# Windowed attention and an MLP mixer on one core: score groups issued one by one instead of in 18 fixed bursts, with new issue orders

## The chip, the cores and the metric

The kernel runs on one core of one Trainium2 chip. The core has a matrix engine (TensorE, in the profile PE, its weight loads PEld), a vector engine (VectorE, DVE), a scalar engine (ScalarE, ACT), a general engine (GpSimd, POOL) and a sequencer that issues transfers (SyncE, SP). The metric is device time in microseconds (us); lower is better. The time given for a kernel is the median of several runs.

## What is computed

Four batches, eight heads, 768 positions, head size 64. Attention keeps, for each query, the first 4 keys (the sinks) and the 128 keys up to its own position. Its result, with the heads side by side as 512 channels, goes through a mixer: a two-layer product over positions (width 256) with a skip connection, then one over channels (width 1536) with another.

```python
scores = scale * np.matmul(q, k.transpose(0, 1, 3, 2))
keep = (pos[None, :] < n_sink) | ((rel >= 0) & (rel < window))     # n_sink 4, window 128
a = softmax(np.where(keep, scores, -1e9))
x = np.matmul(a, v)                        # to [4, 768, 512]
h = np.maximum(x.T @ w_tok1, 0.0) @ w_tok2
u = x + h.T
out = u + np.maximum(u @ w_ch1, 0.0) @ w_ch2
```

## The kernel before

Queries, keys and values are cast to bf16. The 32 heads are worked off as 16 pairs p of two heads, four pairs to a batch. For a pair the scores are computed transposed (keys by queries) in three groups g of two key tiles each, as three diagonal stripes of the window. Each group fills a slot of two PSUM banks, of which there are two (`sc`); four more banks (`mx`) serve everything else. ACT takes the exponential, DVE or POOL masks it, and PE multiplies it with the values.

**Units.** All work of PE is cut into units, each a short run of matmuls whose results other engines then fetch. A unit is named by a letter and a number; the letters are streams:

- first phase (pairs 0 to 3, batch 0): `t` transposes q and k, `m` writes the mask into PSUM, `s` scores, `o` products with the values (and one product with the sinks, o0), `g` and `h` the token mixer of batch 0 (two mix_h units, three mix_u units, three transpositions in each).
- later (pairs 4 to 15): `a` scores and what goes with them, `v` products with the values (two units a pair, v0 and v1 for pair 4), `k` the token mixer of batches 1 to 3, `c` the first channel product (c0 to c23 for batch 0, 42 units for each other batch), `x` and `y` the second channel product.

The string `ORDERED` lists all units in the order in which PE gets them; `plan.run` walks through it. PE executes in that order and no other, so a unit whose operands are late holds up all units behind it.

**The planner.** All other operations (copies out of PSUM, exponentials, masks, transfers) are put into the program between the units by `class Plan`, when the kernel is built: it keeps a clock for each engine, adds fixed costs, and emits the operation that can begin first. The times in it only decide the order of instructions on DVE, ACT, POOL and SP and on which of them an operation goes; on the chip each instruction waits for its own operands. For a load it takes a landing time: the queue's own time plus `RECEIPT`, and it lets `LANES` loads be on their way before the next is issued. `choose` picks PSUM banks for a unit and keeps, in `held`, who reads them.

**Loads.** The string `LOADS` gives the order in which POOL issues the loads from pair 4 on: `q4`, `k4`, `v4` and so on of a pair, `t1` and `t2` the token weights `w_tok1` and `w_tok2`, `c0` to `c3` quarters of `w_ch1`, `d0` to `d3` quarters of `w_ch2`. One queue takes them in that order. For pairs 8 to 15 q and k are transposed by a DMA that SP issues (line 542) once the load has landed; for pairs 4 to 7 PE transposes them.

**Forms.** A score matmul of pairs 4 to 15 has 64 rows and 64 columns of weights ("quarters": four run side by side), a sink product 64 by 32 ("eighths"), the first phase's scores 64 by 128 ("halves"); all else is 128 by 128 ("full"). The planner charges `SWITCH` for a change of form.

**Bursts.** In the stream `a` of before, a0 and a1 are the transpositions of q and k of pair 4. The 36 score groups of the 12 later pairs are taken two by two, which gives a2 to a19: a burst holds the transposition of the next pair by quarters (pairs 5 to 7), two groups, and the sink product of two pairs or the transposition of a batch's u by quarters where one falls due, sorted by form. So a burst needs both `sc` slots. In program order:

```python
for n in range(0, len(groups), 2):
    pieces = [x for k in range(3) for g in groups[n:n + 2] for x in (g[k] if k != 1 else [g[k]])]
    pieces.sort(key=lambda x: x.form)
    units.append(burst(*pieces))
```

Nearly all matmuls go through one helper and have line 187; transpositions have lines 158, 162, 190 and 584. Other lines: 172 loads of q and k (pairs 8 on), 180 of v, 205 of weights; 680 the exponential; 691 and 699 masks; 196 copies by DVE or POOL; 194 copies by ACT; 1471 and 1509 sums of weights; 1216 sums of the hidden layer; 1262 sums into the output tile.

Of the kernel before, what the change touches and what calls it, by code (L numbers as in the profile page):

```python
# [17 lines left out]
def kernel(  # L18
# [43 lines left out]
    )  # L62
    LOADS = (
        "q4 v1 t1 k4 v2 t2 v3 k5 q5 k6 q6 c0 v4 c3 c2 v5 q7 v6 k7 q9 c1 k9 q8 d3 k8 d1 v7 v11 d0 k10 d2 v8 "
        "k11 v10 v9 q10 k13 q11 q13 k12 q12 q15 v12 q14 k14 k15 v14 v13 v15 "
# [25 lines left out]
    LATER = "cxyakv"  # L91
# [204 lines left out]
    LANES = 8  # L296
# [3 lines left out]
    RECEIPT = 1500.0  # L300
    BIAS = 400.0
# [6 lines left out]
    class Op:  # L308
        def __init__(self, cost, fn, deps=(), then=(), size=0.0, lag=None, loads=0, traffic=0.0):
# [6 lines left out]
            self.need = {}  # L316
            self.first = self.last = 0
# [7 lines left out]
    class Plan:  # L325
# [57 lines left out]
        def other(self):  # L383
            best = None
            queue = False
            for n, op in enumerate(self.pending):
# [10 lines left out]
                e = min(op.cost, key=lambda e: max(self.free[e], r) + op.cost[e] + BIAS * (e == "DVE"))  # L397
                t = max(self.free[e], r)
# [6 lines left out]
        def commit_pe(self, op, t):  # L405
            given.update(self.choose(op)[1])
            for tag, banks in op.need.items():
                for n, readers in zip(given[tag], banks):
                    for m in (2 * n, 2 * n + 1) if tag == "sc" else (n,):
                        self.held[m] = readers  # L410
# [14 lines left out]
        def run(self, units, early):  # L425
# [3 lines left out]
            while units or self.pending:  # L429
# [3 lines left out]
                if o is not None and (t is None or o[0] <= t):  # L433
# [3 lines left out]
                    op.done = self.free[o[2]] + op.lag  # L437
                    if op.traffic:
# [572 lines left out]
    def attention_and_tokens():  # L1011
# [9 lines left out]
        units += [turn(first, n) for n in range(2)]  # L1021
        for p in range(first, last + 1):
# [3 lines left out]
            with_first, with_second = [], []  # L1026
            if p + 1 < min(BY_DMA, last + 1):
                with_first.append(transposed(p + 1))
            groups.append((with_first, scores(p, 0), [], sink_rows(p)))
            if p % 2:  # L1030
                groups[-1][2].append(sinks.pop())
            groups.append(([], scores(p, 1), with_second, None))
            groups.append(([], scores(p, 2), [], None))
            if p % 2 == 0:
                sinks = [score_sinks(p + 1)]
            if hp == NHP - 1 and p < BY_DMA:
                groups[-1][2].append(turned_u(b, 0))
# [548 lines left out]
```

## Time and profile before

| what | value |
|---|---|
| median of 3 runs | 195.54 us (192.81 to 198.23) |
| the profiled execution | 194.1 us, of it the span of its instructions 192.1 us |
| PE matmul busy | 180.8 us, 94% of the span, 2270 instructions |
| DVE busy | 161.1 us (84%) |
| ACT busy | 109.1 us (57%) |
| POOL busy | 81.9 us (43%) |
| granted TensorE clock | 1.0 throughout |

Times in the profile count from the first instruction of the span. A row of the timeline gives the start, the time from the start of the first to the end of the last instruction of the group, the engine, line, operation, out<-in with the shape of the weights and of the moving operand, the count, and in brackets the engine's idle time before it with what released it. Matmuls are pipelined: a row is longer than the time for which it keeps the next one from starting, so start times are compared, not lengths.

### The profile page before, as it was taken

What the parts mean: (1) busy time and instruction counts of PE and PEld (TensorE: products, weight loads), DVE (VectorE), ACT (ScalarE), POOL (GpSimd) and SP (SyncE); (2) the same over time, 40 slices, a digit from 0 to 9 for tenths busy, and PEclk for the clock granted to TensorE, in tenths of its full rate; (3) what the DMA queues carried; (4) which work ended last, traced back from release to release, by engine and by line L of the source; (5) the groups of instructions that cost most, each with busy time, mean ns of one, the idle gap of its engine ahead of it and who ended that gap; (6) DMA issues with size and microseconds to landing.
All of it is one profiled execution on the core that took longest, in us unless ns stands there. A gap on an engine that the chain in (4) does not pass through costs nothing.

```text
span 192.1 us, 5590 instructions
## 1 busy us (share of the span) xinstructions
PE 180.8 (94%) x2270; PEld 132.9 (69%) x2273; DVE 161.1 (84%) x340; ACT 109.1 (57%) x205; POOL 81.9 (43%) x132
## 2 busy tenths in 40 slices
PE   6688979799999999999999999999999999999992
PEld 1345667467667778885776789876777887667881
DVE  4466667697999799999999999989999986699953
ACT  4698858998896551528955760767453111773000
POOL 7198856497865398994262493040000000000000
PEclk9999999999999999999999999999999999999999
DMA  5999999999999999999999996250211204400144
GB/s 177 252 309 193 187 197 194 178 179 173 152 167 151 122 116 144 167 143 281 158 147 125 151 116 136 109 218 3 58 29 27 55 3 164 164 3 0 55 138 139
DMA packets 82601, 26.32 MB, mean 137 GB/s; under 512 B 70032, under 2 KB 80272, under 8 KB 82576
## 3 DMA queue, kind: packets, MB, share of 16 engines
q0 software_dynamic: 56864, 11.80, 77.6%
q1 hardware_dynamic: 25136, 13.64, 36.3%
q10 hardware_dynamic: 576, 0.52, 0.8%
q8 instruction: 18, 0.29, 0.6%
q14 instruction: 7, 0.06, 0.1%
HBM read 26.75 MB, written 6.29 MB: 172 GB/s over the span
## 4 chain that ended last, share of the span: by engine, by line
PE 60%; DMA 30%; DVE 3%; POOL 2%; issue 2%; SPq 0%
PE ps L187 60%; DMA w_ch<-in_moe_w_ch_dram 19%; DMA q_f<-in_q_dram 7%; DMA w_tok<-in_moe_w_tok_dram 4%; DVE q_f L1471 1%; DVE v_sums L1216 1%; POOL k_bf L172 1%; DVE o_sb L1262 1%; POOL v_aug L180 1%; DVE pT L699 1%; POOL w_ch L205 1%; SPq L135 0%; POOL q_bf L196 0%; PE ps L584 0%
## 5 line engine op out<-in xcount | busy, mean ns | idle before, releaser
L680 ACT ACTIVATE pT<-ps 128x1024 bf16<-128x1024 f32 (+1 forms) x48 | 44.0, 956 | 13.7 <-PE ps L187 13.6
L194 ACT ACTIVATE parts<-ps 128x384 f32<-128x384 f32 x54 | 24.4, 493 | 26.7 <-PE ps L187 22.5
L187 PE MATMUL ps<-uT,w_ch 128*128 128x384 bf16 x168 | 34.0, 326 | 0.1
L187 PEld LDWEIGHTS <-v1T 128*128 128x128 bf16 x288 | 27.8, 98 | 5.9 <-DVE q_f L1471 0.5
L1150 DVE CUSTOM_DVE_ANT_0 v1T<-ps,parts 128x384 bf16<-128x384 f32 x54 | 28.6, 552 | 3.4 <-PE ps L187 2.5
L187 PEld LDWEIGHTS <-w_ch 128*128 128x128 bf16 x204 | 19.3, 98 | 11.0 <-issue 0.6
L200 ACT ACTIVATE v1T<-ps 128x384 bf16<-128x384 f32 x39 | 18.9, 495 | 8.6 <-PE ps L187 8.0
L187 PEld LDWEIGHTS <-v_sums 128*128 128x128 bf16 x216 | 20.8, 98 | 3.0 <-issue 0.6
L187 PE MATMUL ps<-uT_sums,k_f 128*128 128x384 bf16 x108 | 22.6, 326 | 0.0
L187 PEld LDWEIGHTS <-w_tok 128*128 128x128 bf16 x192 | 18.4, 98 | 4.4 <-issue 0.5
L691 POOL TENSOR_SCALAR_AFFINE_SELECT pT<-pT 128x256 bf16<-128x256 bf16 (+1 forms) x28 | 15.0, 569 | 13.4 <-issue 9.3
L180 POOL DMA_DIRECT2D v_aug<-in_v_dram x16 | 17.0, 1063 | 7.0 <-PE ps L187 3.6
L187 PE MATMUL ps<-q_f,v1T 128*128 128x256 bf16 x144 | 19.2, 273 | 0.3 <-DVE q_f L1471 0.2
L187 PEld LDWEIGHTS <-k_f 128*128 128x128 bf16 x144 | 13.7, 98 | 7.7
L187 PE MATMUL ps<-w_ch,v1T 128*128 128x256 bf16 x144 | 19.0, 273 | 0.0
L187 PE MATMUL ps<-v_aug,pT 128*128 128x65 bf16 x352 | 18.0, 194 | 1.0 <-DMA v_aug<-in_v_dram 1.0
L1262 DVE TENSOR_TENSOR o_sb<-ps,u_sb 128x512 f32<-128x512 f32 (+1 forms) x32 | 17.1, 548 | 1.9 <-PE ps L187 1.9
L187 PEld LDWEIGHTS <-pT 128*128 128x128 bf16 x352 | 16.1, 98 | 3.2 <-DMA v_aug<-in_v_dram 1.3
L187 PE MATMUL ps<-q_f,v_sums 128*128 128x256 bf16 x144 | 18.2, 273 | 0.2 <-DVE o_sb L1262 0.2
L769 DVE TENSOR_TENSOR x_sb<-ps,recip 128x384 bf16<-128x384 f32 x32 | 17.3, 552 | 0.6
L1262 DVE TENSOR_TENSOR o_sb<-ps,o_sb 128x256 f32<-128x256 f32 (+1 forms) x24 | 12.9, 551 | 3.4 <-PE ps L187 3.2
L172 POOL DMA_DIRECT2D k_bf<-in_k_dram x16 | 13.4, 840 | 5.0 <-DMA q_bf<-in_q_dram 2.7
(88 smaller groups left out, 293.3 us busy)
## 6 DMA issues: line engine op xcount, KB each, us to landing
v_aug<-in_v_dram POOLq DMA_DIRECT2D x16, 192.0 KB, 11.0
w_ch<-in_moe_w_ch_dram POOLq DMA_DIRECT2D x8, 384.0 KB, 10.0
out_dram<-o_sb SPq DMA_DIRECT2D x6, 512.0 KB, 2.8
out_dram<-o_sb SPq DMA_DIRECT2D x10, 256.0 KB, 2.8
q_f<-in_q_dram SPq DMA_DIRECT2D x4, 384.0 KB, 6.5
k_f<-in_k_dram SPq DMA_DIRECT2D x4, 384.0 KB, 6.8
q_bf<-in_q_dram POOLq DMA_DIRECT2D x16, 96.0 KB, 8.3
k_bf<-in_k_dram POOLq DMA_DIRECT2D x16, 96.0 KB, 10.7
```

The source lines that it names most:

```text
L172: in_order(nc.gpsimd.dma_start(out=out[:, h], in_=rows[:, h]))
L180: in_order(nc.gpsimd.dma_start(out=v_aug.rearrange("p i t d -> p (i t) d")[:, :, 0:D], in_=v[b].rearrange("h s d -> (h s) d")[2 * hp * S:2 ...
L187: issue(nc.tensor.matmul(*args, skip_group_check=True, **kwargs))
L194: in_order(nc.scalar.activation(out, in_, AF.Copy))
L200: in_order(nc.scalar.activation(out, in_, AF.Relu))
L205: return in_order(nc.gpsimd.dma_start(out=out, in_=in_))
L680: in_order(nc.scalar.activation(part(tiles["pT", p][:, :, ds(2 * g, 2)]), of_keys(tiles["ps_s", p, g])[:, :, 0:width(g)], AF.Exp, scale=scale,
L691: in_order(nc.gpsimd.affine_select(out=pt, in_=pt, compare_op=ALU.is_ge, fill=0.0, base=-n, pattern=[[0, nk], [1 - 2 * n, P]], channel_mul ...
L699: in_order(nc.vector.tensor_tensor(out=pt, in0=pt, in1=m, op=ALU.min))
L769: in_order(nc.vector.tensor_tensor(out=x_sb[b][:, ts(half, QH), ts(hp, 2 * D)].rearrange("p t (i d) -> p t i d", i=2), in0=tiles["ps_o", p ...
L1150: in_order(nc.vector._custom_dve(TENSOR_ADD_SAT, out=v1_of(i, half), in0=ps, in1=kept[:, n], s0=HUGE, s1=0.0,))
L1262: in_order(nc.vector.tensor_tensor(out=sb(*out), in0=tiles["ps_out", b, t0, key[0]], in1=in1(), op=ALU.add,))
```

## The change

Each score group becomes a unit of the stream `a` (now a0 to a35, three to a pair). The transpositions by quarters get a stream `w` of their own: w0 and w1 for q and k of pair 4, w2, w3 and w4 for pairs 5 to 7, w5 and w6 for u of batch 1 (first and second half of its channels). The six sink products of two pairs become the stream `n`. The matmuls stay the same. `ORDERED` and `LOADS` are new strings.

In the planner `LANES` goes from 8 to 7, `RECEIPT` from 1500 to 2100 ns, and readers of one PSUM bank get a common record `reads`: an operation on another engine than the bank's last reader is taken to begin no earlier than 60 ns after that one's end.

```diff
@@ -46,23 +46,24 @@
 
 
     ORDERED = (
-        "t0-1 m0-1 s0-1 t2 m2 s2 t3 m3 s3 o0 m4 s4 t4 m5 o1 s5 t5 o2 m6 s6 t6 m7 s7 t7 o3 m8 s8 o4 a0 s9-10 m9 "
-        "g0-1 m10 a1 s11-12 o5-6 g2 o7-8 g3 a2 h0-1 g4-6 h2-3 a3 h4-6 g7 h7 c15 c0 c5 c10 a4 v0-1 c9 c6 c22 "
-        "v2-3 a5 c8 k0 c16 c7 c11 c3 c23 k1-2 a6 k3 c13 c1-2 c14 c18-19 a7 v4 c12 c20 v5 c17 v6 c21 v7 a8 x0 c4 "
-        "x1 k4 y0 a9 y2 x6-7 y3-4 x2 k5-6 x10 y5 x3 k7 v8 y6 x4-5 a10 x11 x8 c31 c24 x9 x12-13 v9-10 c27 c33 "
-        "c26 y1 c32 c29 v11 c34-35 a11 c28 c45 c36-37 c30 c47 c25 a12 c46 k8 c49 c48 a13 v12 c50 v13 c51 c41 "
-        "c38 k9 c39 c43 c40 c59 k10 v14-15 c52 c61 c42 c62 c54 c53 c63-64 c44 k11 c55-56 c65 c60 k12 c58 a14 "
-        "c57 x14 k13 x15 x18 a15 x19-21 a16 x22 y7 x24 k14 x25 v16 k15 x23 y8 x26-27 y9 v17 a17 v18 y10-11 v19 "
-        "a18 y12 x16-17 c73 a19 v20 y13 k16 c67 c66 c69 c75 v21 c76 c68 c77 c83 c71 c80 c78-79 c70 c82 c74 k17 "
-        "c81 c72 c85 k18 c94 c87 c84 c88 v22-23 c89 c86 k19 c96-97 c95 c90-91 k20 c101 c99 c92 c98 k21 c103-104 "
-        "c93 x28 c105 c100 c106 k22 c102 k23 y15 c107 x29 x32 y14 c115 x30-31 x34 x33 y17 x35 y16 c108 x36-39 "
-        "y19 c118 c117 y18 x40-41 y20 c119 c109 c111 c120 c110 c116 c113 c122 c132 c112 c129 c124 c130 c121 "
-        "c131 c114 c134 c125 c123 c126 c133 c136 c143 c127-128 c137 c145 c138 c135 c144 c139 c146 c140 c147 "
-        "x42-43 c141-142 c149 x44 x48 c148 x46 y21 x45 x47 x49 y24 y22 x50 x52-53 x51 y23 y26 x54-55 y27 y25"
+        "t0-1 m0-1 s0-1 t2 m2 t3 s2 m3 o0 s3 m4 s4 t4 o1 m5 s5 t5 o2 m6 t6 s6 m7 s7 t7 o3-4 m8 s8-10 w0 m9 g0 "
+        "m10 w1 s11-12 o5-6 g1 a0 o7 w2 a1-2 o8 g2-4 h0 g5 h1 a3 g6-7 h2-3 n0 h4-6 a4 v0-1 h7 c0 c5 c8 w3 a5 c3 "
+        "c7 c2 c18 a6 w4 a7 v2 c17 v3 c16 c20 c23 n1 c13 c21 a8-9 c15 k0 c22 c1 a10-11 c19 c12 c10 k1 c14 k2 "
+        "c11 c6 v4 k3 v5 x0-1 c4 v6 c9 v7 x2 a12-13 y0 k4 x3 x6 y3 y2 x7 a14 n2 a15 y5 y4 a16 k5 x10 v8 w5 a17 "
+        "x4-5 x11 v9 y6 y1 k6 x12 k7 v10-11 a18 w6 x13 c24 x8 c31 a19-20 k8 c26 x9 c34 c33 c32 c27 c36 c35 c25 "
+        "n3 a21 c28 k9 c29 c37 c39 c38 v12 a22 v13 k10 c30 c45 c40 c46 a23 c41 v14 c47 c59 c42 c48 c43 c49 v15 "
+        "c50 k11 c61 c44 c52 c51 c60 c62-63 c54 c53 c64 c55 k12 c57 c56 x14 k13-15 c65 c58 a24 x15-16 n4 a25-26 "
+        "y7 x17 x20 y8 x21 y10 y9 a27-28 x18-19 v16-17 y11-12 x24 v18 x25 y13 a29-30 x22 x26 c66 a31-32 x27 c73 "
+        "x23 c68 c67 v19 c74 c70 c75 c69 n5 a33 c77 c76 c71 k16 v20 c78 c80 a34 v21 c79 c72 k17 c87 c82 c88 c81 "
+        "k18 a35 c90 v22 c83-84 c89 c94 c92 v23 c85 c96 c91 c86 c101 k19-20 c102-103 c97 c93 c98 c104-105 x30 "
+        "c100 c106 c99 c95 x28 k21 c107 k22 y15 k23 x29 y14 c108 x32 x34 x31 x33 c115 x35 y17 y16 x36 x38-39 "
+        "y18-19 x37 x40 c118 x41 c110 c117 y20 c109 c120 c111 c122 c112 c116 c119 c113 c125 c124 c114 c123 c121 "
+        "c129 c127 c136 c132 c130 c126 c131 c137 c134 c143 c128 c133 c139 c138 c144-146 c135 c141 c140 c147 x42 "
+        "c148 x43-44 c142 c149 x46 x48 y21 x45 y22 x47 x49 y23-24 x50 x52-53 y25-26 x54-55 y27 x51"
     )
     LOADS = (
-        "q4 v1 t1 k4 v2 t2 v3 k5 q5 k6 q6 c0 v4 c3 c2 v5 q7 v6 k7 q9 c1 k9 q8 d3 k8 d1 v7 v11 d0 k10 d2 v8 "
-        "k11 v10 v9 q10 k13 q11 q13 k12 q12 q15 v12 q14 k14 k15 v14 v13 v15 "
+        "q4 v1 t1 v2 k4 v3 k5 q5 t2 c0 k6 v4 k7 c2 v5 q6 c1 q7 c3 d3 d2 d0 d1 q8 k8 v6 v7 k9 q9 v8 v9 k10 q10 "
+        "v10 k11 q11 k12 v11 k13 q12 q13 v12 k14 q14 k15 v13 q15 v14 v15 "
     )
     ORDER = (1, 2, 7, 6, 4, 5, 3)
     NQ = 6
@@ -88,7 +89,7 @@
 
     psum = ctx.enter_context(tc.tile_pool(name="psum", bufs=1, space=bass.MemoryType.PSUM))
     NSC, NMX = 2, 4
-    LATER = "cxyakv"
+    LATER = "cxyakvwn"
 
     given = {}
 
@@ -293,11 +294,11 @@
     PE_OUT = 200.0
     SWITCH = 95.0
     FIRST = 1800.0
-    LANES = 8
+    LANES = 7
     TURN, STORE = 1300.0, 700.0
     CROWDED = 1.7
     BLOCK = 1.4
-    RECEIPT = 1500.0
+    RECEIPT = 2100.0
     BIAS = 400.0
     FETCH, FETCH_ALONE = 7200.0, 4600.0
 
@@ -314,6 +315,7 @@
             self.urgent = 0
             self.loads, self.traffic = loads, traffic
             self.need = {}
+            self.reads = []
             self.first = self.last = 0
             self.after = None
 
@@ -394,8 +396,11 @@
                     r = max(r, self.landings[len(self.landings) + op.loads - LANES - 1])
                 if r is None:
                     continue
-                e = min(op.cost, key=lambda e: max(self.free[e], r) + op.cost[e] + BIAS * (e == "DVE"))
-                t = max(self.free[e], r)
+                at = {
+                    e: max([self.free[e], r] + [x[1] for x in op.reads if x[0] != e]) for e in op.cost
+                }
+                e = min(op.cost, key=lambda e: at[e] + op.cost[e] + BIAS * (e == "DVE"))
+                t = at[e]
                 if best is None or t < best[0] - 1e-6 or (
                     t < best[0] + 1e-6 and e == best[2] and op.urgent > self.pending[best[1]].urgent
                 ):
@@ -406,6 +411,9 @@
             given.update(self.choose(op)[1])
             for tag, banks in op.need.items():
                 for n, readers in zip(given[tag], banks):
+                    last = [None, 0.0]
+                    for r in readers:
+                        r.reads.append(last)
                     for m in (2 * n, 2 * n + 1) if tag == "sc" else (n,):
                         self.held[m] = readers
             first = count[0]
@@ -435,6 +443,8 @@
                     op.fn(o[2])
                     self.free[o[2]] = o[0] + op.cost[o[2]]
                     op.done = self.free[o[2]] + op.lag
+                    for x in op.reads:
+                        x[:] = [o[2], self.free[o[2]] + 60.0]
                     if op.traffic:
                         behind = max(0.0, self.queue - self.free["SP"])
                         crowded = behind > 1000.0
@@ -1018,23 +1028,23 @@
             tokens.extend(mix_u(b, g, st, 2) for st in range(0, NT, 2))
 
         prepare(first)
-        units += [turn(first, n) for n in range(2)]
+        turned = [turn(first, n) for n in range(2)]
         for p in range(first, last + 1):
             b, hp = pairs[p]
             if p < last:
                 prepare(p + 1)
-            with_first, with_second = [], []
+            with_second = []
             if p + 1 < min(BY_DMA, last + 1):
-                with_first.append(transposed(p + 1))
-            groups.append((with_first, scores(p, 0), [], sink_rows(p)))
+                turned.append(burst(transposed(p + 1)))
+            groups.append((scores(p, 0), [], sink_rows(p)))
             if p % 2:
-                groups[-1][2].append(sinks.pop())
-            groups.append(([], scores(p, 1), with_second, None))
-            groups.append(([], scores(p, 2), [], None))
+                groups[-1][1].append(sinks.pop())
+            groups.append((scores(p, 1), with_second, None))
+            groups.append((scores(p, 2), [], None))
             if p % 2 == 0:
                 sinks = [score_sinks(p + 1)]
             if hp == NHP - 1 and p < BY_DMA:
-                groups[-1][2].append(turned_u(b, 0))
+                groups[-1][1].append(turned_u(b, 0))
             out += [pv(p, half) for half in range(2)]
             if hp == 1 and p > NHP + 1:
                 tokens_of(b - 1, 1)
@@ -1043,12 +1053,14 @@
             if hp == 2:
                 tokens_of(b, 0)
         tokens_of(pairs[last][0], 1)
-        for n in range(0, len(groups), 2):
-            pieces = [x for k in range(3) for g in groups[n:n + 2] for x in (g[k] if k != 1 else [g[k]])]
-            pieces.sort(key=lambda x: x.form)
-            units.append(burst(*pieces))
-            units[-1].then.extend(g[3] for g in groups[n:n + 2] if g[3] is not None)
-        return units, tokens, out
+        sunk = []
+        for scored, others, rows in groups:
+            units.append(burst(scored))
+            if rows is not None:
+                units[-1].then.append(rows)
+            for x in others:
+                (turned if x.form == QUARTERS else sunk).append(burst(x))
+        return units, tokens, out, turned, sunk
 
     def mix_channels(b):
         units = []
@@ -1526,7 +1538,7 @@
     plan.pending.append(done["masks"])
 
     streams = dict(zip("smtohg", first_attention()))
-    streams.update(zip("akv", attention_and_tokens()))
+    streams.update(zip("akvwn", attention_and_tokens()))
     for b in range(B):
         for name, mixed in zip("cxy", mix_channels(b)):
             streams.setdefault(name, []).extend(mixed)
```

## The prediction

> **What bounds the kernel now.** I read the page's busy shares and slices first, then the chain that ended last, then the timeline of PE around every place where its starts are not evenly spaced.
>
> ```profile
> PE 180.8 (94%) x2270; PEld 132.9 (69%) x2273; DVE 161.1 (84%) x340; ACT 109.1 (57%) x205; POOL 81.9 (43%) x132
> PE   6688979799999999999999999999999999999992
> DMA  5999999999999999999999996250211204400144
> ```
> ```profile
> 50.01 16.86 DMA w_ch<-in_moe_w_ch_dram
> ...
> 73.10 5.32 PE ps L187 x65
> ...
> 78.85 109.67 PE ps L187 x1097
> ...
> 188.55 0.43 DVE o_sb L1262
> ```
>
> PE is busy in every slice and, from 73.1 us to 188.5, it is the chain by itself: more than 1,100 matmuls with nothing between them. There a unit can be put earlier or later without any gain, as long as PE never waits. Before that the chain is transfers (the last quarter of `w_ch2` lands at 66.9), and the PE slices fall below 9. So only two things can move the time: waits of PE before 73 us, and matmul time itself. The latter has a fixed part and a part that the order sets, the changes of form.
>
> The waits are found by comparing starts with the pace at which matmuls follow each other.
>
> ```profile
> 24.70 0.38 PE L187 MATMUL ps<-h1T,w_tok 128*128 128x256 bf16 x2
> 26.08 0.36 PE L187 MATMUL ps<-v_aug,pT 128*128 128x65 bf16 x6 [1.00 <-DMA v_aug<-in_v_dram]
> ...
> 27.75 0.38 PE L162 MATMUL ps<-ident,q_bf 64*64 64x64 bf16 x24
> ...
> 28.14 0.53 PE L187 MATMUL ps<-qT,kT 64*64 64x256 bf16 x16
> ```
> ```profile
> 32.27 0.56 PE L162 MATMUL ps<-ident,q_bf 64*64 64x64 bf16 x24
> ...
> 34.01 0.61 PE L187 MATMUL ps<-h1T,w_tok 128*128 128x256 bf16 x4
> 35.46 0.40 PE L190 MATMUL ps<-ident,u_sb 128*128 128x128 bf16 x4 [0.84 <-ACT qT L194]
> 36.18 0.83 PE L190 MATMUL ps<-ident,u_sb 128*128 128x128 bf16 x12 [0.32 <-DVE u_sb L919]
> 37.08 2.76 PE L187 MATMUL ps<-uT,w_ch 128*128 128x384 bf16 x16
> ```
> ```profile
> 50.67 0.49 PE L187 MATMUL ps<-h1T,w_tok 128*128 128x256 bf16 x3
> 51.10 0.52 PE L187 MATMUL ps<-qT,kT 64*64 64x192 bf16 x16
> 51.54 0.40 PE L187 MATMUL ps<-qT,kTs 64*32 64x512 bf16 x4
> 51.87 0.61 PE L187 MATMUL ps<-h1T,w_tok 128*128 128x256 bf16 x4
> ```
> ```profile
> 66.17 0.62 PE L187 MATMUL ps<-qT,kT 64*64 64x192 bf16 x16
> ...
> 67.51 0.83 PE L187 MATMUL ps<-q_f,v1T 128*128 128x256 bf16 x6 [0.22 <-DVE q_f L1471]
> 68.18 2.13 PE L187 MATMUL ps<-q_f,v_sums 128*128 128x256 bf16 x18
> 70.43 0.81 PE L187 MATMUL ps<-q_f,v1T 128*128 128x256 bf16 x6
> 71.25 0.81 PE L187 MATMUL ps<-w_ch,v1T 128*128 128x256 bf16 x6
> 71.90 1.04 PE L187 MATMUL ps<-h1T,w_tok 128*128 128x256 bf16 x8
> 73.10 0.27 PE L187 MATMUL ps<-q_f,v_sums 128*128 128x256 bf16 x1 [0.16 <-DVE o_sb L1262]
> ```
>
> Pace: six matmuls of 256 columns take 71.90 - 71.25 = 0.65, so 0.108 each; one of 128 columns is taken as half of that, 0.054. Now the waits, each a distance of starts less the work in it:
>
> - 24.70: 2 x 0.108 = 0.22, next start 1.38 later: **1.16**, for the values of pair 3.
> - 32.27 to 34.01 is 1.74. The 48 transpositions take 28.14 - 27.75 = 0.39, scores and sinks 51.87 - 51.10 = 0.77: **0.58**, within one burst that needs both score slots.
> - 34.01 to 35.46, four matmuls: **1.02**; to 36.18, four short ones: **0.50**; to 37.08, twelve: **0.25**. The transpositions of the token mixer wait, first until ACT has copied the transposed q of this burst out of a bank, then for the mixer's own results.
> - 66.17 to 67.51 against the same 0.77: **0.57**; 67.51 to 71.25, 30 matmuls (3.24): **0.50**; 71.90 to 73.10, eight (0.87): **0.33**. These are the first users of the last `w_ch2` pieces and of their sums.
>
> Together 4.9 us. That is the most that a better order could win from these places.
>
> **The change part by part.**
>
> *More changes of form.* Going by the strings, with the bursts taken apart into their forms, the old order changes form 68 times on PE, the new one 83 times (29 stretches of small matmuls become 37; n0 and n1 stand alone, n2 lies between two groups). The price is in the rows above: three full matmuls from 50.67 fill 0.32, the quarters start at 51.10, so going in costs 0.11. The last form starts at 51.54, its four sink products of 512 columns run side by side in 2 x 0.108, and the full matmul starts at 51.87: coming out costs 0.11. So 15 x 0.11 = **+1.65 us**, and this falls on PE where nothing hides it. Above it could be at most what a matmul shows beyond its columns: 0.40 long against 0.22 streamed, 0.18, so 15 x 0.18 = 2.7.
>
> The Trainium skill (TensorEngine Tiling (Array Packing), Tiling Modes) says that changing the tiling mode, not merely the tile, drains the engine, which speaks against the change; the rows agree with a cost but show 0.11 us. By the latency formula of TensorE: Matmul & The Clock Gate, Single matmul latency (398 cycles besides the columns, at 2.4 GHz), a full drain would be 0.166 us as an estimate, and the sum 0.8 us later.
>
> *Where the waits go.* In the new string o7 (values of pair 3) comes after a0 and g1, and v3 is loaded ahead of t2 instead of behind it, 2.0 us earlier by the rate below: the 1.16 goes. No transposition of q and k stands among h2 to h7 any more (w3 comes after c8), n0 lies between h3 and h4, and a4, v0 and v1 (1.2 us) ahead of h7: the 1.02, 0.50 and 0.25 go. A group no longer asks for two score slots at once: the 0.58 goes. The four `d` loads come as 20th to 23rd instead of within 24th to 31st; the last of them lands some 2.4 ahead of k8 (53.6 below), at 51, and x0, its first user, starts 4.2 ahead of a12 (62.2 below), at 58: the 0.57, 0.50 and 0.33 go. **-4.9 us.** I take all of it; the lower bound of this gain is nothing, if what comes next in order is late instead.
>
> *What is late next, early.* Loads are in one queue.
>
> ```profile
> 24.00:32.00 8.00, 7.00 (x150) 5.92 (x147) 5.24 (x15) 5.22 (x11) 4.45 (x6) 1.00 1.51 194
> 48.00:56.00 8.00, 8.00 (x70) 4.99 (x68) 7.61 (x15) 6.91 (x14) 6.99 (x11) 1.00 1.89 159
> ```
> ```profile
> v_aug<-in_v_dram POOLq DMA_DIRECT2D x16, 192.0 KB, 11.0
> w_ch<-in_moe_w_ch_dram POOLq DMA_DIRECT2D x8, 384.0 KB, 10.0
> ...
> w_tok<-in_moe_w_tok_dram POOLq DMA_DIRECT2D x2, 384.0 KB, 7.6
> ```
>
> The last column of the first two rows is GB/s. At 194 a load of 384 KB takes 2.0 us, one of 192 KB 1.0. Before, q5 landed by 27.75 at the latest (its transposition starts then), with t2 ahead of it. In the new order t2 comes behind q5: so q5 by 25.7 and t2 by 27.7. When are they wanted? g2, which needs t2, starts at 24.3 before (the two matmuls at 24.70 are its last). In front of it now stand in addition o7 and o8 (0.9), a0, a1 and a2 (together about 0.5), w2 (0.4) and, net of a merged stretch, one entry and exit (0.2): 26.3. So PE can wait up to 1.4 there, most of it already at w2; nothing, if t2 lands as much earlier as its queue had slack. All units are behind that wait. I take **+1.0 us**, nearer to the upper end, since sizes and rate are rows.
>
> *What is late next, at pair 8.* q8 comes 24th instead of 23rd, and k8 stays 25th, but of the first 25 loads three small ones (v6, q9, k9: 576 KB) are replaced by three large (d0, d1, d2: 1152 KB).
>
> ```profile
> 49.90 1.80 SPq L542 DMA_TRANSPOSE kT<-k_bf  x1
> ```
> ```profile
> 59.87 0.43 POOL L196 COPY kTs<-kT 64x4 bf16<-64x4 bf16 x2 [1.48 <-DMA kT<-k_bf]
> ...
> 65.42 0.82 POOL L172 DMA_DIRECT2D q_bf<-in_q_dram x1 [2.92 <-DMA k_bf<-in_k_dram]
> ```
> ```profile
> DMA to landing us min/median/max: 6.0/8.8/10.4
> ```
>
> Before, k8 was there at 49.9, when SP issued its transposition, and that landed 10 us later. 576 KB more at 159 GB/s are 3.7 us, so k8 at 53.6, and transposed between 59.6 and 64.0 (the last row is of the tile kT). Its first reader is a12.
>
> ```profile
> 61.66 0.54 PE L187 MATMUL ps<-qT,kT 64*64 64x256 bf16 x16
> ```
>
> Pair 8's scores began at 61.66 before. Without the waits ahead of them (3.5), with x0 to x2 (2.0), one more c unit of four 384-column matmuls (0.65), and seven more changes of form net of one transposition of u that comes later (0.4), they stand at 61.2, with the early wait at 62.2. So PE waits 0 to 1.8 there; I take **+0.5**. What is queued behind it is y0, k4 and all else. Pair 9 (a15, some 6.4 later) has v6, v7, k9 and q9 loaded in between: 768 KB, 5.1 us, so its transposition is about as tight; it shares that term.
>
> *ACT.* a0 to a2 come up to 3 us earlier, when ACT still has pair 3's exponentials. Bounds 0 and one exponential, 1.0; I take nothing, since each of these units now needs one slot. *Reads of one bank.*
>
> ```profile
> DVE kTs L196 <- ACT kT L194: 5.9, 6, 1.5
> ```
>
> The planner now knows that a copy on DVE waits for ACT's read of the bank; that is 5.9 us of DVE idle time, beside PE work, so I count nothing for it but a part of the waits already counted. `LANES` and `RECEIPT` act only through the order.
>
> **Sum.** Span 192.1 - 4.9 + 1.65 + 1.0 + 0.5 = 190.35; with the 2.0 us outside the span (194.1 - 192.1), **192.4 us**. The median of before, 195.5, lies 0.7% above its profiled execution, and its three runs spread by 2.8%; so 2% is about what this kernel's measurement can tell from no change, and 192.4 is 1.6% below that median.
>
> **The rivals.**
>
> 1. *No new waits.* Loads keep up, both terms (1.5) vanish: 190.9, and about 0.5 of small waits that I left in the ledger may go too: 190.4. For it: PE shows none after 73 us. Against: every early wait here was made by a load. Chance 0.22.
> 2. *The waits move.* As many as were removed return elsewhere: 194.1 + 1.65 = 195.7. For it: the transfers are busy throughout that part (DMA slices 9), and both orders load the same bytes. Against: the new string has more independent work between dependent units. Chance 0.20.
> 3. *Slower: pair 9's transposition.* With transpositions in the queue, POOL stood 2.92 us for the landing of one small k load (above). Two such holes among the four loads up to q9 put it at 53.6 + 5.1 + 5.8 = 64.5 and its transposition at 74.5, against a15 at 68.6: with the early 1.0, 6.9 us of new waits, 194.1 - 4.9 + 1.65 + 6.9 = 197.8. It decides once new waits pass 3.25, that is, when this transposition lands after 70.9. Chance 0.13.
> 4. *A change of form costs 0.18*, so +2.7: 193.5. The rows speak against it. Chance 0.05.
>
> My forecast has the other 0.40, with its own range of 190.9 to 194.5.
>
> **Numbers.** Over 2% faster is below 191.6: rival 1 and 0.12 of the forecast, 0.34. Over 2% slower is above 199.4: the upper half of rival 3 and the scatter of rivals 2 and 3, 0.10. Between: 0.56. The range takes rival 1 at its lower end with some scatter, 189.5, and most of rival 3, 197.5.
>
> **What would show it.** After: about 83 changes of form with the same 0.11; no wait of PE at h5 to h7 nor at the first x and y units; a wait of about 1 us for q5 or `w_tok2` before 28 us; one below 2 us at pair 8's or 9's first scores, for the transposing DMA; from some 75 us on PE alone in the chain. I am wrong if PE still waits 4 us or more in total, above all between 60 and 75 us, or if c, x and y units run dry after 80 us, where the new order puts pairs 12 to 15 later.

## The result, and the profile after

The changed kernel takes **192.07 us** (median of 14 runs, 191.36 to 194.38), the kernel before in the same comparison 194.2 us (14 runs). The ratio is 0.9899, with a 95% interval of 0.9873 to 0.9926: 1% faster, below the 2% of the prediction's own bound. Predicted were 192.4 us. The profiled execution took 191.36 us with a span of 189.6; before it was 194.1 with 192.1. The profiled one is the fastest of the 14, while that of before (194.1) lies near its median, so the two profiles differ by 2.7 us and the medians by 2.1. All ratios below are to the kernel before, with the 95% interval in brackets; where some runs of a kernel stand apart from the rest at a longer time and a lower granted clock (the units alone, the merged units, `RECEIPT` alone: the profiled execution is one of these), the ratio is taken without them.

The page's busy shares and slices first:

```profile
PE 182.7 (96%) x2273; PEld 132.8 (70%) x2273; DVE 159.0 (84%) x335; ACT 111.0 (59%) x213; POOL 75.0 (40%) x120
PE   6899999999999999999999999999999999999991
DMA  5999999999999999999999994250210306200234
```

Before, five of PE's second to eighth slices were below 9; now only the second is, and from the third on PE is full to the end, with the same transfers. The chain that ended last (start, length, what) says the same:

```profile
22.14 2.93 PE ps L188 x57
...
41.07 30.11 PE ps L188 x346
71.18 0.51 PE ps L594 x48
...
78.90 106.64 PE ps L188 x1028
185.57 0.69 DVE o_sb L1274
```

Line 187 of the old file is line 188 of the new. Before, a transfer of `w_ch2` stood in the chain from 50 to 67 us; now matmuls fill it from 41 us on. The last row shows what became worse: the kernel now ends with x51, whose sum covers 512 columns (0.69 us) instead of 256 (0.43), and whose output transfer is larger.

The waits of PE, as the view of waits lists them (who waited for what: total us, times, longest), are all in the first 20 us. The view lists times in which PE stands empty; smaller losses within a group are found from starts, below.

```profile
PE ps L188 <- DVE kT L217: 1.5, 1, 1.5
PE ps L188 <- ACT pT L690: 0.7, 2, 0.4
PE ps L159 <- DVE k_bf L197: 0.2, 1, 0.2
PE ps L159 <- ACT q_bf L195: 0.2, 1, 0.2
```

Now PE's timeline at the places where the prediction found its waits, and where it expected new ones.

```profile
23.47 0.82 PE L188 MATMUL ps<-x_sb,w_tok 128*128 128x256 bf16 x6
24.22 0.38 PE L188 MATMUL ps<-qT,kT 64*64 64x256 bf16 x8
24.53 0.36 PE L188 MATMUL ps<-v_aug,pT 128*128 128x65 bf16 x6
...
25.00 0.62 PE L163 MATMUL ps<-ident,q_bf 64*64 64x64 bf16 x24
...
26.05 0.23 PE L188 MATMUL ps<-v_sink,pT_sink 128*128 128x130 bf16 x1
...
26.60 0.27 PE L188 MATMUL ps<-x_sb,ident 128*128 128x256 bf16 x1
26.71 0.38 PE L188 MATMUL ps<-h1T,w_tok 128*128 128x256 bf16 x2
...
32.92 0.61 PE L191 MATMUL ps<-ident,u_sb 128*128 128x128 bf16 x8
33.46 0.36 PE L188 MATMUL ps<-qT,kT 64*64 64x192 bf16 x8
33.75 0.36 PE L188 MATMUL ps<-v_aug,pT 128*128 128x65 bf16 x6
...
60.38 0.82 PE L188 MATMUL ps<-w_ch,v1T 128*128 128x256 bf16 x6
61.13 0.55 PE L188 MATMUL ps<-qT,kT 64*64 64x256 bf16 x16
61.60 0.83 PE L188 MATMUL ps<-w_ch,v1T 128*128 128x256 bf16 x6
...
67.20 0.40 PE L188 MATMUL ps<-qT,kTs 64*32 64x512 bf16 x4
```

Three readings. *The price of a group of its own:* the six matmuls from 23.47 are done 0.65 later, at 24.12, and the next full matmul starts at 24.53, so the single group g0 costs 0.41; from 32.92 + 8 x 0.054 = 33.35 to 33.75 the single g1 costs 0.40; the pair of both, from 61.03 to 61.60, costs 0.57. Two stretches instead of one cost 0.24 here (0.22 with the starts unrounded), that is, **0.11 for a change of form**. *The early wait:* the unit w2 with a1 and a2 runs from 24.90 to 26.05, 1.14 us. In the kernel before the same transpositions with the first two groups of a pair took 0.95; a1 and a2 are the last two, 0.05 shorter (0.52 against 0.57 where such pairs of groups stand alone, at 50.2 and 61.0 us). So 0.24 is lost there, not 1.0, and it isn't a wait for a load: q5 was issued at 17.80 and landed 6.3 us later, at 24.1, and in six other runs (2, 3, 4, 5, 11 and 12) the same unit takes the same 1.14 to 1.15, though it starts 0.3 to 1.3 us later. The trace names no cause. `w_tok2`, issued at 18.51, landed at 26.0, before its first reader at 26.71, which runs at pace (the two rows from 26.60). *Pair 8:* the scores a12 and a13 start at 61.13 at the pace of the full matmuls before them; there is no wait.

SP's and POOL's timelines show why. SP issued the transposition of pair 8's k at 51.77 (53.6 was predicted for k8) and that of pair 9's at 56.93. The copies of the sink keys `kTs`, which wait for them, ran on POOL at 58.6 for pair 8 and 64.1 for pair 9, before a12 (61.13) and before n2 (67.20), pair 9's first reader.

```profile
51.77 1.22 SPq L552 DMA_TRANSPOSE kT<-k_bf  x1
...
56.93 1.22 SPq L552 DMA_TRANSPOSE kT<-k_bf  x1
```
```profile
58.63 0.42 POOL L197 COPY kTs<-kT 64x4 bf16<-64x4 bf16 x2 [3.40 <-DMA kT<-k_bf]
...
64.09 1.07 POOL L197 COPY kTs<-kT 64x4 bf16<-64x4 bf16 x2 [0.79 <-DMA kT<-k_bf]
...
74.16 0.56 POOL L197 COPY kTs<-kT 64x4 bf16<-64x4 bf16 x2 [3.44 <-DMA kT<-k_bf]
```

Worked out from all of PE's starts, the span's -2.5 us is made of: idle time among full matmuls -2.75; stretches of smaller forms -0.25 (26.88 us in 29 stretches before, 26.63 in 37 now); the tail after the last matmul's start +0.5. The changes of form, counted in the two traces, are 68 and 83. At 0.11 they cost 1.65, so waits within the stretches fell by 1.9, and all waits together by 4.65 (the 0.24 at w2 counted among them).

### The profile page after: what moved, and what is told of

Same layout as the page of the kernel before. It is cut to its first block, busy times and chain, and to the rows that moved or that the text cites. A ratio compares the mean times of both kernels' runs of the same rounds, so it can differ in the third digit from the quotient of the medians.

```text
span 189.6 us, 5582 instructions
## 1 busy us (share of the span) xinstructions
PE 182.7 (96%) x2273; PEld 132.8 (70%) x2273; DVE 159.0 (84%) x335; ACT 111.0 (59%) x213; POOL 75.0 (40%) x120
## 4 chain that ended last, share of the span: by engine, by line
PE 92%; ACT 3%; DMA 2%; DVE 1%; issue 0%; SPq 0%; ACTq 0%
PE ps L188 89%; ACT pT L690 2%; DMA k_f<-in_k_dram 2%; PE ps L163 1%; PE ps L191 1%; PE ps L159 1%; PE ps L594 0%; ACT qT L195 0%; DVE o_sb L1274 0%; DVE k_bf L197 0%; SPq L136 0%; ACT kT L195 0%; ACTq L195 0%; ACTq L690 0%
## 5 line engine op out<-in xcount | busy, mean ns | idle before, releaser
L690 ACT ACTIVATE pT<-ps 128x1024 bf16<-128x1024 f32 (+1 forms) x48 | 45.2, 963 | 19.0 <-PE ps L188 18.4
L195 ACT ACTIVATE parts<-ps 128x384 f32<-128x384 f32 x54 | 25.0, 491 | 21.1 <-PE ps L188 20.1
L188 PE MATMUL ps<-uT,w_ch 128*128 128x384 bf16 x168 | 34.8, 326 | 0.0
L1162 DVE CUSTOM_DVE_ANT_0 v1T<-ps,parts 128x384 bf16<-128x384 f32 x54 | 28.0, 551 | 4.3 <-PE ps L188 3.4
L188 PE MATMUL ps<-uT_sums,k_f 128*128 128x384 bf16 x108 | 23.1, 326 | 0.0
L188 PE MATMUL ps<-q_f,v_sums 128*128 128x256 bf16 x144 | 18.7, 273 | 0.0
L188 PE MATMUL ps<-w_ch,v1T 128*128 128x256 bf16 x144 | 18.5, 273 | 0.0
L188 PEld LDWEIGHTS <-kT 64*64 64x64 bf16 (+2 forms) x343 | 8.1, 105 | 11.2 <-issue 8.2
L188 PE MATMUL ps<-qT,kT 64*64 64x192 bf16 (+2 forms) x336 | 15.6, 252 | 0.1
L1274 DVE TENSOR_TENSOR o_sb<-ps,o_sb 128x512 f32<-128x512 f32 (+1 forms) x24 | 13.1, 553 | 2.7 <-PE ps L188 2.6
```

Of the source, the lines that this page charges most:

```text
L188: issue(nc.tensor.matmul(*args, skip_group_check=True, **kwargs))
L195: in_order(nc.scalar.activation(out, in_, AF.Copy))
L690: in_order(nc.scalar.activation(part(tiles["pT", p][:, :, ds(2 * g, 2)]), of_keys(tiles["ps_s", p, g])[:, :, 0:width(g)], AF.Exp, scale=scale,
L1162: in_order(nc.vector._custom_dve(TENSOR_ADD_SAT, out=v1_of(i, half), in0=ps, in1=kept[:, n], s0=HUGE, s1=0.0,))
L1274: in_order(nc.vector.tensor_tensor(out=sb(*out), in0=tiles["ps_out", b, t0, key[0]], in1=in1(), op=ALU.add,))
```

## The experiments

The question was which part carries the gain: the units, the unit order, the order of loads, or the planner.

**1. New orders, old planner.**

```diff
-    LANES = 7
+    LANES = 8
-    RECEIPT = 2100.0
+    RECEIPT = 1500.0
-        e: max([self.free[e], r] + [x[1] for x in op.reads if x[0] != e]) for e in op.cost
+        e: max(self.free[e], r) for e in op.cost
```

> The changed kernel with its new unit order and load order, but the planner's constants and rules of before (8 lanes, receipt 1500, no record of a bank's readers), so that only the order and engine of the operations beside PE differ. Theory (the gain is PE waits removed by the order of units and loads): as the changed kernel, 191.6 to 192.8 us, no PE wait above 0.5 us after 20 us. Rival (the gain is the stricter planner's placing of copies, exponentials and masks): waits of PE return, 193.5 to 194.5 us.

Measured: 197.39 us, ratio 1.0157 [1.0095, 1.0219], above both ranges. With the old planner the new order loses everything, and 3 us more. In the profiled execution 2 us of that come from its first load of k, which landed at 7.0; in every other trace here it was there by 5.8. The rest is in PE's timeline and waits:

```profile
64.01 0.38 PE L188 MATMUL ps<-qT,kT 64*64 64x256 bf16 x8
65.53 0.36 PE L188 MATMUL ps<-qT,kT 64*64 64x192 bf16 x8 [1.13 <-ACT pT L690]
```
```profile
PE ps L188 <- ACT pT L690: 4.3, 7, 1.2
```

a12 and a13, one stretch of 0.57 us in the changed kernel, now stand 1.13 us apart: the second needs the score slot of the first and waits for its exponential. The planner's choices of banks explain it. The slots of a0 to a35 are, with the new planner and with the old:

```
010100101010010100001000010100101000
010100101010000000000000010100101000
```

From a12 to a24 the old planner gives every group slot 0. Four stretches (at 64, 71, 74 and 86 us) grow by 3.8 us together.

**2. Old planner, but the banks of the changed kernel forced on it**, and **3. the new planner, but the banks of run 1 forced on it.** In both, `BANKS` is a list of the slots and banks of each unit, printed from the other kernel's plan.

```diff
+        for (_, op), word in zip(units, BANKS):
+            sc_banks, mx_banks = word.split("/")
+            op.banks = {"sc": [int(x) for x in sc_banks], "mx": [int(x) for x in mx_banks]}
```

> Planner constants and rules of before with the changed orders, as in the earlier run of that kind, but each unit is given the PSUM banks that it has in the changed kernel. Theory (the 5 us lost there came from pairs of score groups that the old planner put into the same score slot, so that PE waited for the first one's exponential): 192.0 to 193.2 us, no wait of PE for an exponential above 0.5 us after 60 us. Rival (it is the order and engine of copies, exponentials and masks): still 195.5 us or more.

> The changed kernel with its own planner, but each unit is given the PSUM banks that the planner of before chose for these orders (a12 to a24 all in score slot 0). Theory: waits for exponentials at a13, a15, a16 and a20 return, 1.3 + 0.7 + 0.4 + 1.4 = 3.8 us, so 195.3 to 196.5 us. Rival: 192 to 193 us.

Measured: old planner with new banks 194.64 us, ratio 1.0028 [0.9959, 1.0097]; new planner with old banks 199.91 us, ratio 1.0281 [1.0208, 1.0354]. First the old planner with new banks, then the new planner with old banks:

```profile
63.53 0.54 PE L200 MATMUL ps<-qT,kT 64*64 64x256 bf16 x16
```
```profile
PE ps L200 <- ACT pT L713: 1.1, 3, 0.4
PE ps L200 <- ACT uT L207: 0.8, 1, 0.8
```
```profile
64.85 0.38 PE L200 MATMUL ps<-qT,kT 64*64 64x256 bf16 x8
66.36 0.36 PE L200 MATMUL ps<-qT,kT 64*64 64x192 bf16 x8 [1.13 <-ACT pT L713]
```
```profile
PE ps L200 <- ACT pT L713: 3.9, 6, 1.2
PE ps L200 <- DVE u_sb L952: 1.8, 1, 1.8
```

The four waits go with the banks, both ways: with the new banks they vanish (16 matmuls in one row again); with the old ones they return with 3.7 us over the four stretches. Run 3 lost twice what its theory said. (The wait of 1.8 for `u_sb` is another matter: DVE had stood 2.44 us at a `kTs` copy ahead of it. Run 5 takes this up.) So the waits for the slot are caused by the choice of banks. But banks are about half of run 1's 5.3 us: 2.75 were won back, and 2.6 stay, in small waits for copies and exponentials that stand elsewhere on ACT and DVE. Neither theory had this split.

**4. Only the record of reads taken out** (the third edit of run 1 alone).

> The changed kernel without the record of a bank's readers in its planner; score slots come out the same. Theory (no PE wait hung on reads of one bank by two engines): 192.0 to 193.0 us, with DVE waiting again for ACT at kTs. Rival (these waits delay PE): 193.5 us or more.

Measured: 192.66 us, ratio 0.9906 [0.9849, 0.9964], as the theory said. The record is worth nothing that these four runs could tell. The idle time of DVE that the prediction quoted (5.9 us, `kTs` after ACT's `kT`) did fall, to 1.3 us in the changed kernel and 3.8 in this run, and it had been beside PE's work.

**5. Only `RECEIPT` put back.**

```diff
-    RECEIPT = 2100.0
+    RECEIPT = 1500.0
```

> The changed kernel with `RECEIPT` alone put back from 2100 to 1500 ns; orders, `LANES` and the record of reads as changed. The score groups keep the slots that they have in the changed kernel (010100101010010100001000010100101000), but 107 choices of the other banks and the places of many copies differ. Theory (what the planner is worth lies in the score slots): no wait at the four places where the old planner had one slot used twice running, and 192 to 193.5 us. Rival (the other banks and the placing of copies count by themselves, as the run with forced banks suggested): some 1.5 to 3 us of small waits for ACT and DVE, 194 to 195.5 us.

Measured: 194.71 us, ratio 1.003 [0.9983, 1.0076]. The rival's time holds, and the gain is gone, with the score slots unchanged. The profiled execution, at 198.1 us, shows one long wait besides small ones. DVE's timeline, PE's, and the windows (length; busy time of PE, PEld, DVE, ACT, POOL; then the granted clock):

```profile
75.17 0.34 DVE L197 COPY kTs<-kT 64x4 bf16<-64x4 bf16 x2 [2.89 <-DMA kT<-k_bf]
75.54 0.69 DVE L929 TENSOR_TENSOR u_sb<-ps,x_sb 128x512 bf16<-128x512 f32 x1
```
```profile
76.29 2.60 PE L188 MATMUL ps<-q_f,v1T 128*128 128x256 bf16 x12 [2.58 <-DVE u_sb L929]
```
```profile
76.00:80.00 4.00, 3.71 (x20) 2.63 (x20) 3.38 (x8) 0.00 (x0) 0.76 (x1) 0.57 1.80 186
```

Pair 10's transposition ended at about the same time in both kernels: the copies that wait for it start at 74.16 in the changed kernel (on POOL, shown above) and at 75.17 here. In the changed kernel POOL stands idle 3.44 us for it, and PE loses nothing. Here the planner gave the 0.34 us copy to DVE. DVE stood 2.89 us with `u_sb` behind it, PE stood 2.58 us for `u_sb`, and then the granted clock was 0.57 for 4 us. `RECEIPT` is what the planner adds to the landing of a load, not of the transposition; but the transposition can only follow its load, so with the smaller figure the planner expects both 0.6 us earlier. That this is why the copy went to DVE is likely, not shown.

The long wait is probably not what undoes the gain in most runs. Three of the 11, this one among them, took 198.1 to 198.2 us with a mean clock of 0.99; the other eight took 193.5 to 194.9, six of them with 0.998 to 1.0. The wait of 2.58 and the clock of 0.57 after it (4 x 0.43 = 1.7) make 4.3 us, about the distance between the two. Without them the profile is still some 2.4 us above the changed kernel, in small pieces, as the rival had it: 0.7 before w2, 0.6 at pair 8's first scores, 0.3 at 54.6 us, 0.5 in the tail. That the other eight lost the same pieces is an estimate from this one trace.

**6. The changed kernel with the old order of loads** (`LOADS` of before).

> The changed kernel with the load order of before. Theory (order of units and loads belong together): v3 comes behind w_tok2 again, 1.5 us too late for o7, and the w_ch2 pieces at 59 and 67 us instead of about 50, while x0 to x3 are asked for from 56 us on: PE waits 6 to 9 us in all, 197.5 to 201 us. Rival (units of their own are enough, PE finds other work): below 193.5 us.

Measured: 199.09 us, ratio 1.0249 [1.0188, 1.0311], within the theory's bounds. PE's waits name the loads, and the windows show the clock at 0.58 after the longest of them, which ended at 43.75:

```profile
PE ps L188 <- DMA w_ch<-in_moe_w_ch_dram: 2.2, 1, 2.2
...
PE ps L188 <- DVE v_sums L1228: 1.1, 1, 1.1
PE ps L163 <- DMA q_bf<-in_q_dram: 1.1, 1, 1.1
```
```profile
44.00:48.00 4.00, 4.00 (x86) 2.65 (x85) 2.48 (x6) 2.43 (x6) 2.17 (x3) 0.58 1.51 150
```

**7. The kernel before with the new order of loads.**

> The kernel before with the new load order alone. Theory (unit order and load order belong together): the waits from 66 to 73 us go (1.4) and that at 25 us, but k6, q6, q7 and w_tok2 come later than the old unit order asks for them, 2 to 6 us of new waits: 195 to 199 us. Rival (the load order is the gain): 191.5 to 192.8 us.

Measured: 201.55 us, ratio 1.0387 [1.0324, 1.045], slower than either theory had it. That the loads are the gain is excluded. q and the token weights come too late for the old order:

```profile
PE ps L162 <- DMA q_bf<-in_q_dram: 2.5, 1, 2.5
PE ps L187 <- DMA w_tok<-in_moe_w_tok_dram: 1.9, 1, 1.9
```

**8. The kernel before with the new planner** (`LANES`, `RECEIPT` and the record of reads).

> The kernel before with its own orders and bursts, but the stricter planner (7 lanes, receipt 2100, record of readers). Theory (the waits hang on the order of units and loads, which is the old one): 193.3 to 195.5 us, PE waits before 74 us still above 3 us. Rival (the stricter planner alone is the gain): 191.5 to 192.8 us.

Measured: 198.15 us, ratio 1.018 [1.0115, 1.0244]. Theory and rival both missed: the new planner by itself makes the old order slower, by waits of about 1 us each for sums and transfers.

```profile
PE ps L187 <- DVE v1T L1225: 1.3, 1, 1.3
PE ps L187 <- DVE q_f L1480: 1.2, 1, 1.2
PE ps L187 <- DMA w_ch<-in_moe_w_ch_dram: 1.0, 1, 1.0
```

**9. The split units alone**: each burst of before taken apart in its place (a2 as `w2 a0 a1`, a3 as `w3 a2 a3 n0`, and so on), with the loads and the planner of before. PE's order of work stays, with 68 changes of form.

> Units of their own alone: the changed code with the old planner constants and rules and the old load order, and the units of each old burst put side by side at the burst's place, so that PE's order is that of before (68 changes of form). Theory (the gain lies in the new orders): 193.3 to 194.6 us; at most the 0.58 us of the burst at 32 us goes. Rival (the units themselves free PE, because a group no longer asks for two score slots): 191.5 to 192.8 us.

Measured: of 12 runs three at 193.05, 193.56 and 195.59 us, the others from 198.34 to 200.57; ratio 0.9996 [0.9932, 1.0061], by the three lowest. Smaller units alone bring nothing even there, and in nine of 12 runs the kernel takes some 4 to 6 us more than before. The profiled execution is one of these nine, and shows a wait and what follows it:

```profile
PE ps L189 <- DMA kT<-k_bf: 3.9, 1, 3.9
```
```profile
64.00:72.00 8.00, 5.89 (x49) 4.26 (x50) 4.82 (x10) 2.69 (x4) 4.47 (x8) 0.79 2.35 129
```

PE waited 3.88 us at pair 8's first scores, until 66.1, for one of two transpositions that SP issued at 50.6 and 52.5, and then got a clock of 0.79 over 8 us. This is the mechanism of the prediction's third rival, one pair earlier, in a kernel with the old order of loads.

**10. More changes of form**: seven units moved by one place, so that groups that stood side by side stand apart (a11, a13, a20, a26, a28, a30, a32). 97 changes instead of 83.

```diff
-"... a10-11 c19 ... a12-13 y0 ... a19-20 k8 ..."
+"... a10 c19 a11 ... a12 y0 a13 ... a19 k8 a20 ..."
```

> The changed kernel with seven pairs of neighbouring score groups (a10 a11, a12 a13, a19 a20, a25 a26, a27 a28, a29 a30, a31 a32) parted by the unit that followed them: 14 more changes of form (97), same matmuls. Theory (0.11 us each, nothing hides them): 14 x 0.11 = 1.5, so 193.3 to 193.9 us. Rival 1 (a change is hidden by weight loads ahead): 192.1 us. Rival 2 (a full drain of 0.166 to 0.18 each): 194.4 to 194.6 us.

Measured: 194.81 us, ratio 1.0024 [0.9988, 1.006]; 2.74 above the changed kernel (2.4 by the two ratios), 1.5 expected. PE's starts show 0.22 for each of the seven splits, 1.54 in all, as expected. The rest stands in the profile as 0.6 for sums at 111 us, 0.55 at w2 and just behind it, and 0.2 in the tail. Up to 50 us PE's order is that of the changed kernel, so the 0.55 belongs to the transfers of this execution and not to the moved units. So the price is confirmed by itself; the total is not that price alone.

**11. Fewer changes of form**: five units moved beside neighbours of their form (n1, n2, a16, a23, a35), 75 changes.

> The changed kernel with five units moved beside a neighbour of their form (n1 before a8, n2 after a15, a16 before w5, a23 after a22, a35 after a34): 75 instead of 83 changes of form. If a change costs 0.11 and the moves open no new waits: 192.07 - 0.9 = 191.2 us. Rival (the order is in step with the planner's banks and slots, and any move opens waits of PE of 1 to 4 us): 192.5 to 195 us.

Measured: 201.27 us, ratio 1.0319 [1.0253, 1.0385], 9.2 us above the changed kernel, where eight changes less should have brought 0.9. Again a `kTs` copy had been given to DVE, which stood at it until 61.8; `x_sb` was behind it, and PE waited. DVE's timeline, PE's waits, and the windows:

```profile
61.83 0.34 DVE L198 COPY kTs<-kT 64x4 bf16<-64x4 bf16 x2 [3.41 <-DMA kT<-k_bf]
```
```profile
PE ps L189 <- DVE x_sb L780: 4.4, 2, 3.3
```
```profile
64.00:68.00 4.00, 4.00 (x47) 2.93 (x46) 2.48 (x6) 1.35 (x2) 1.65 (x4) 0.66 1.68 134
```

**12. y27 last instead of x51** (x51 moved to before x52).

```diff
-"... x50 x52-53 y25-26 x54-55 y27 x51"
+"... x50-53 y25-26 x54-55 y27"
```

> The changed kernel with x51 moved from the last place to before x52, so that the last unit is y27, whose sum and store are half as large. Theory (the end after the last matmul grew from 3.7 to 4.2 us because x51 ends the order): 0.3 to 0.5 us less, 191.6 to 191.8 us, with 3.7 us behind the last matmul. Rival (the earlier stores keep the queue, whatever comes last): 192.1 us.

Measured: 191.98 us, ratio 0.9887 [0.9836, 0.9938]. In the profile the end after the last matmul is 3.96 us against 4.22, half of what the change had added; in the total that can't be told from the changed kernel's 192.07. No version here beats the changed kernel measurably.

**Taken together.** Every piece alone costs time or brings nothing: units ±0 at best, loads +3.9%, planner +1.8%, new orders without the planner +1.6%, without the loads +2.5%. The gain of 1% belongs to the set. The parts are tied through the static program: an order decides when a transfer is wanted, the planner decides which bank a unit gets and which engine is parked at a transfer, and one misplaced wait of 1 to 4 us is as large as all that the change wins. What was not tried is `LANES` alone, and a new search for an order under the old planner; so it stays open whether the new planner is better, or only the one for which this order was made. That run 8 is slower and run 1 too speaks for the latter.

## Why the prediction was right

- **What bounds the kernel** was right: PE, its waits before 73 us, and its changes of form. After the change the chain is PE's alone from 22 us on, the waits are gone, and nothing after 80 us runs dry.
- **Waits removed, -4.9:** all eight listed places run at pace. Net of the 0.24 at w2 the fall is 4.65, so 4.9 went, against 4.9. This term held.
- **Changes of form, +1.65:** 68 and 83 were counted in the traces, at 0.11 each, and seven splits in run 10 cost 0.22 each. This term held; rival 4 (0.18) is out. A full drain of 0.166, as the Trainium skill's latency formula would give (TensorE: Matmul & The Clock Gate, Single matmul latency, an estimate), is above what the rows show.
- **The new early wait, +1.0: mis-sized.** No wait for a load was there; the 0.24 at w2 is something else. The step that failed is the landing of the two loads. PE's side was right: it came to g2 at 26.60, which without the 0.24 is the predicted 26.3. But q5 landed at 24.1 instead of 25.7 and `w_tok2` at 26.0 instead of 27.7, both before they were wanted. The prediction took the start of a transposition (27.75, "at the latest") for the landing of q5 before, which was at 27.2, and in that kernel v3 had landed 2.8 us behind `w_tok2` (23.2 and 26.0) where the rate gives 1.0; the estimate carried this delay into the new order.
- **The wait at pair 8 or 9, +0.5: mis-sized.** None was there. Pair 8's scores came at 61.13, and the prediction had 61.2 without the early wait. But k8 was transposed from 51.77 instead of 53.6, 1.9 us later than before instead of 3.7, and the copies ran 2.5 and 3.1 us before the first readers. The term lay within its bounds of 0 to 1.8. Rival 3 (pair 9's transposition at 74.5) was far off for this kernel, where pair 9 was ready at 64.1. But its mechanism is real and close by: the profiled executions of runs 3, 5, 9 and 11 each lost 1.8 to 3.9 us to a late transposition, directly or through DVE, the last three with the lower clock on top. (In its sum, 768 KB at 159 GB/s are 4.9 us, not 5.1; nothing hangs on it.)
- **The tail, counted as nothing:** +0.5 in the profile. The diff showed that x51 with 512 columns would end the order; run 12 took half of the 0.5 back by that alone.
- **Reads of one bank, counted as nothing:** right, by run 4. **`LANES` and `RECEIPT` "act only through the order":** true, but the prediction gave them no price, and in run 5 putting back `RECEIPT` alone undoes the whole gain.

The sum: predicted -4.9 + 1.65 + 1.5 = -1.75 on the span, measured -4.65 + 1.65 + 0.5 = -2.5. The new waits were 1.3 too high and the tail 0.5 too low. The share outside the span was 1.8 instead of 2.0. So of the listed cases the trace bears out rival 1 (loads keep up, no new waits; chance 0.22) and not the forecast's own story, in which both waits come. That the median of 192.07 lies only 0.3 below the 192.4 predicted is in part luck: the profiled execution, for which the sum was made, took 191.36, 1.0 below it.

## What to carry to other kernels

Before a larger static order is believed, price its waits from start times, not from busy shares: here both traces show PE 94 to 96% busy, and the whole gain was in eight holes of 0.25 to 1.2 us. In a program whose engines run in order, give a small operation that waits for a late transfer to the engine on which nothing urgent depends; the same copy cost PE nothing on POOL and 2.6 us on DVE, in the two executions that were traced. And test the parts of such a change also together with an order made for them: here each part alone was worth nothing or less.

## What was not expected of the hardware

- **After a longer wait of PE its clock was often lower for some 4 us.** A wait of 2.58 us was followed by a clock of 0.57 over 4 us (run 5), 3.29 by 0.66 over 4 us (run 11), 3.88 by 0.79 over 8 us (run 9): 4 x 0.43, 4 x 0.34 and 8 x 0.21 are 1.4 to 1.7 us more. In run 6 a wait of 2.2 us was followed by 0.58 over 4 us, and in run 1 one of 2.3, until 7.7, by 0.57 from 8 to 12 us. It isn't a fixed rule: in run 7 the wait of 2.5 us, until 36.1, left the clock at 1.0, and so did one of 1.8 in run 3. In the profile of the changed kernel no wait is longer than 1.5 us, and its clock is 1.0 throughout.
- **A transposition by DMA that is issued while loads are under way took long, and unevenly**: in the changed kernel those issued at 51.77 and 56.93 were ready at 58.6 and 64.1, some 7 us later; in run 9 one issued at 52.5 at the latest was ready at 66.1, over 13.
